# Output scaling on one engine and its sums on another, in a sketched attention and expert attention kernel

## The chip, the cores and the metric

The kernel runs on one core of a Trainium2 chip. The metric is the time on the device in microseconds (us). Before the change it was 341.58 us, the median of three runs (339.06 to 341.63).

The engines are named as the profile names them: PE is TensorE (matmuls; PEld its weight loads), DVE is VectorE, ACT is ScalarE, POOL is GpSimd, and SP is SyncE, which here only issues transfers. They run side by side, each through its own instructions in order, and wait for one another by semaphores. SBUF is the working memory, of 128 partitions. PSUM holds the results of the matmuls[...].

## The reference

Two blocks follow one another. The first is an attention whose queries and keys are sketched to 64 features; its output is the input `x` of the second, a causal attention with four experts, of which each token uses the best two.

```python
# 4 batches, 4 heads, 1088 tokens, head size 32, sketch size r = 8
def phi(x):
    a = np.einsum('rd,bhsd->bhsr', S1, x)
    b = np.einsum('rd,bhsd->bhsr', S2, x)
    return np.einsum('bhsi,bhsj->bhsij', a, b).reshape(*x.shape[:-1], r * r)
q_p, k_p = phi(q), phi(k)
kv = np.einsum('bhsf,bhsd->bhfd', k_p, v)
z = np.sum(k_p, axis=2)
num = np.einsum('bhsf,bhfd->bhsd', q_p, kv)
den = np.einsum('bhsf,bhf->bhs', q_p, z)[..., None] + 1e-06
attn_out = num / den                     # then (B, S, 128) as x

# 4 experts, expert size 64; w: shares of the best two experts of each token
...
for e in range(4):
    q = x @ wq[e]; k = x @ wk[e]; v = x @ wv[e]
    scores = scale * (q @ k.transpose(0, 2, 1))
    scores = np.where(causal, -1e9, scores)
    scores = scores - scores.max(-1, keepdims=True)
    a = np.exp(scores)
    a /= a.sum(-1, keepdims=True) + 1e-09
    ye = a @ v @ wo[e]
    for kk in range(2):
        out += (topk[:, :, kk] == e)[..., None] * w[:, :, kk:kk + 1] * ye
```

## The kernel before

All is float32. The four batches are pipelined: while a batch goes through the expert attention, the first block of the next batch is put between. The expert attention of a batch is a list of units. A unit holds the scores of up to two blocks of 128 queries and one pair of experts (index `g`, two pairs); two units with the same 256 queries (index `p`) make one output. A last unit has the 64 remaining queries.

Per unit, TensorE makes scores (`sc`), VectorE adds the mask and takes the maximum (`take`, L460), ScalarE makes exponentials and their sums `z` (`soften`, L466), TensorE turns the exponentials in blocks (`tp`, L86), these are copied out of PSUM (`aT`), TensorE multiplies them with the values (`av`, L590), the result is copied out (`yT`) and multiplied with the output weights (`po`, L662). A copy out of PSUM goes to VectorE or ScalarE by an account of the work booked on each:

```python
given = {"v": 0, "a": 0}
def evacuate(out_, in_, lean=-0):
    n = math.prod(in_.shape[1:])
    if given["v"] + lean + 70 < given["a"]:
        give("v", n + 100)
        nc.vector.tensor_copy(out_, in_)          # L74
    else:
        give("a", n + 30)
        nc.scalar.copy(out_, in_)                 # L77
```

The products of the sketch. In the first batch VectorE makes them, in the others GpSimd, in two pieces (`j0` to `j1` is 0 to 4 and 4 to 9), that is 1024 and 1280 columns:

```python
def sketch(nm, xT_, j0, j1):
    ...                                           # two sketches per token into abS (kab, qab)
    ab = abS[nm][:, :, j0:j1].rearrange("p x j h r -> p x (j h) r")
    n = H * (j1 - j0)
    with tc.issue_after(fps["turned"].ins) if first else nullcontext():
        ins = (nc.vector if first else nc.gpsimd).tensor_tensor(          # L293: kp, qp
            out=fps[nm][:, j0:j1].rearrange("p j h (x y) -> p (j h) x y", y=R),
            in0=ab[:, 1, :, None, :].to_broadcast([128, n, R, R]),
            in1=ab[:, 0, :, :, None].to_broadcast([128, n, R, R]),
            op=ALU.mult)
```

The share of an expert, divided by its sum of exponentials, is one number per token and expert:

```python
def shares(name, z, gws):
    r = p4.tile([128, 2, E], F32, tag="r", ...)
    nc.vector.tensor_scalar_add(r, z, 1e-9)                               # L556
    nc.vector.reciprocal(r, r)                                            # L557
    nc.vector.tensor_tensor(out=r, in0=r, in1=gws, op=ALU.mult)           # L558
    return r
```

It is made where the second unit of an output makes its values, just ahead of the `av` matmuls, and used when the output is made:

```python
def values():
    share = None if g < NG - 1 else shares(f"{b}_{p}", z, gw[:, 2 * p : 2 * p + 2])
    av = bank(f"av{name}")
    ...                                                                   # matmuls, L590
    evacuate(yT[:, g], av[:, 0:256])
    return [] if g < NG - 1 else [lambda: output(b, p, yT, share)]

def output(b, p, yT, share):
    nq, n = (128, 2) if p < NJ // 2 else (64, 1)
    final = b == B - 1 and p == 0
    pos = [bank(...) ... for e in range(2)]       # a bank for each expert of a pair
    acc = p2.tile([128, 2, NG, DM], F32, tag="acc", ...)[0:nq, 0:n]       # two buffers
    ...                                           # matmuls po, L662
    for g, x in [(g, x) for g in range(NG) for x in range(n)]:
        s0, s1 = (share[:, x, 2 * g + e : 2 * g + e + 1] for e in range(2))
        give("a", 260)
        give("v", 260)
        nc.scalar.activation(out=acc[:, x, g], in_=pos[0][:, x, g], func=ACTF.Copy, scale=s0)    # L668
        nc.vector.scalar_tensor_tensor(out=acc[:, x, g], in0=pos[1][:, x, g], scalar=s1,         # L669
                                       in1=acc[:, x, g], op0=ALU.mult, op1=ALU.add)
    ...
    for x in range(n) if final else [slice(0, n)]:
        eng = nc.vector if final else nc.gpsimd
        eng.tensor_tensor(out=ob[:, x], in0=..., in1=..., op=ALU.add)     # L675: sum over the pairs
        nc.sync.dma_start(out=tokens[:, x], in_=ob[:, x])
```

The order of VectorE's and ScalarE's instructions is that of the text, and comes from this loop over units (`done` are outputs, `tiled` and `cols` are parts of the next batch, such as sketches):

```python
made[0], exps = make(0)                           # scores, first block
emit(turns + rows); emit(exps)
made[1], exps = make(1)                           # scores, second block
emit(done)                                        # the output that came due
emit(tiled)
emit(exps[0:1]); emit(cols[0:2]); emit(exps[1:]); emit(cols[2:])
done = [f for values in group for f in values()]  # shares and values of the unit before
group = values
...
```

Of the kernel before, what the change touches and what calls it, by code (L numbers as in the profile page):

```python
# [10 lines left out]
F32 = mybir.dt.float32  # L11
# [8 lines left out]
def kernel(  # L20
# [201 lines left out]
    def prepare(b):  # L222
# [40 lines left out]
        def sketch(nm, xT_, j0, j1):  # L263


            if nm not in abS:
                abS[nm] = p2.tile([128, 2, NJ, H, R], F32, tag="ab", name=f"{nm}ab{b}")
                fps[nm] = p2.tile([128, NJ, H, R * R], F32, tag="fp", name=f"{nm}p{b}")

            w, parts = (32, NS) if first else (32 * NS, 1)  # L270
            ts = [bank(f"{nm}ps{b}_{j0}_{m}") for m in range(2)]
            for j in range(j0, j1):
                for m in range(2):
                    for half in (0, 64):
                        rows, x = slice(64 * m, 64 * m + 64), 128 * j + half
                        for s in range(parts):
                            nc.tensor.matmul(ts[m][half : half + 64, w * (j - j0) : w * (j - j0) + w],
                                             xT_[rows, x : x + 64],
                                             SKW[rows].rearrange("p s x h r -> p (s x h r)")[:, w * s : w * s + w],
                                             start=(s == 0), stop=(s == parts - 1))  # L280
            for m in range(2):
                t = ts[m][:, 0 : w * (j1 - j0)].rearrange("p (j s x d) -> p s x j d", j=j1 - j0, x=2, d=2 * R)
                part = abS[nm][:, :, j0:j1, 2 * m : 2 * m + 2].rearrange("p x j h r -> p x j (h r)")
                give("a", 16 * (j1 - j0) + 60)
                nc.scalar.copy(part, t[:, 0])
                if w > 32:
                    give("v", 16 * (j1 - j0) + 100)
                    nc.vector.tensor_tensor(out=part, in0=part, in1=t[:, 1], op=ALU.add)

            ab = abS[nm][:, :, j0:j1].rearrange("p x j h r -> p x (j h) r")  # L290
            n = H * (j1 - j0)
            with tc.issue_after(fps["turned"].ins) if first else nullcontext():
                ins = (nc.vector if first else nc.gpsimd).tensor_tensor(  # L293
                    out=fps[nm][:, j0:j1].rearrange("p j h (x y) -> p (j h) x y", y=R),
                    in0=ab[:, 1, :, None, :].to_broadcast([128, n, R, R]),
                    in1=ab[:, 0, :, :, None].to_broadcast([128, n, R, R]),
                    op=ALU.mult)
            if first:
                mark[0] = ins.ins

# [261 lines left out]
    def units(b, qk, vt, gw):  # L562

        of_tiles = {}

        def tiles(p):
            if p not in of_tiles:
                of_tiles[p] = (p2.tile([128, NG, 256], F32, tag="yT", name=f"yT{b}_{p}"),  # L570
                               p4.tile([128, 2, E], F32, tag="z", name=f"z{b}_{p}"))
            return of_tiles[p]

        def weights(p, g):
            return p2.tile([128, 16 * 256], F32, tag="aT", name=f"aT{b}_{p}_{g}")

        def group(p, g, aT):
            yT, z = tiles(p)
            nk = 2 * (2 * p + 2)
            aT = aT[:, 0 : nk * 256].rearrange("p (e j s) -> p e j s", e=2, s=256)  # L580
            name = f"{b}_{p}_{g}"

            def values():
                share = None if g < NG - 1 else shares(f"{b}_{p}", z, gw[:, 2 * p : 2 * p + 2])
                av = bank(f"av{name}")
                for j in range(2 * p + 2):
                    lo = 128 * max(0, j - 2 * p)
                    for e in range(2):
                        c = HD * (2 * g + e)
                        nc.tensor.matmul(av[HD * e : HD * e + HD, lo:256], vt[:, j, c : c + HD],  # L590
                                         aT[:, e, j, lo:256], start=(j == 0), stop=(j == 2 * p + 1))

                evacuate(yT[:, g], av[:, 0:256])
                if g < NG - 1:
                    return []
                return [lambda: output(b, p, yT, share)]

            def make(x):
                return scores(b, 2 * p + x, g, qk, z[:, x, 2 * g : 2 * g + 2])

            def turns(made, x):
                return turns_of(f"{name}_{x}", 2 * p + x, made[x], aT, 128 * x)

            return "P" if p == 1 else "G", make, turns, [values]

        def first_group():
            yT, z = tiles(0)
            aT = weights(0, 0)
            four = [group(0, g, aT[:, 4 * 256 * g :]) for g in range(NG)]
            return ("Q", lambda x: scores_first(b, qk, [z[:, :, 2 * g : 2 * g + 2] for g in range(NG)]),  # L610
                    lambda made, x: [f for g in range(NG) for i in range(2) for f in turns_of(
                        f"{b}_0_{g}_{i}", i, made[0][g][i], aT[:, 4 * 256 * g :][:, 0 : 4 * 256].rearrange(
                            "p (e j s) -> p e j s", e=2, s=256), 128 * i)],
                    [four[g][3][0] for g in range(NG)])

        large = [(p, g) for p in ((1, 2, 3) if b < B - 1 else (1, 3, 2)) for g in range(NG)]
        last_at = large.index((3, 1))
        if b < B - 1:
            yield first_group()
        last_at = large.index((3, 1))  # L620
        for n, (p, g) in enumerate(large):
            yield group(p, g, weights(p, g))
            if n == last_at:
                yield last_unit(b, qk, vt, gw)
        if b == B - 1:
            yield first_group()

    def last_unit(b, qk, vt, gw):
# [3 lines left out]
        z_all = p4.tile([64, 1, E], F32, tag="z8a", name=f"za{b}_8", bufs=2)  # L632
        yT = p2.tile([128, NG, 256], F32, tag="yT", name=f"yT{b}_8")

        def values():
            av = bank(f"av{b}_8")
            for g in range(NG):
                for j in range(NJ):
# [4 lines left out]
                                         aT[0:m, e, j, 64 * g : 64 * g + 64], start=(j == 0), stop=(j == NJ - 1))  # L643

            evacuate(yT[:, :, 0:64], av[:, 0:128].rearrange("p (g s) -> p g s", g=NG))
            for g in range(NG):
                nc.vector.tensor_copy(z_all[:, 0, 2 * g : 2 * g + 2], z[64 * g : 64 * g + 64])
            share = shares(f"{b}_8", z_all, gw[0:64, NJ - 1 : NJ])
            return [lambda: output(b, NJ // 2, yT, share)]

        return ("L", lambda x: scores_last(b, qk, z), lambda made, x: turns_of(f"{b}_8", NJ - 1, made[0], aT, 0), [values])

    def output(b, p, yT, share):

        nq, n = (128, 2) if p < NJ // 2 else (64, 1)
        final = b == B - 1 and p == 0
        pos = [bank(f"po{b}_{p}_{e}").rearrange("p (x g d) -> p x g d", x=2, g=NG)[0:nq] for e in range(2)]
        acc = p2.tile([128, 2, NG, DM], F32, tag="acc", name=f"acc{b}_{p}")[0:nq, 0:n]
        for g, x in [(g, x) for g in range(NG) for x in range(n)]:
            for e in range(2):  # L660
                rows = slice(64 * e, 64 * e + 64)
                nc.tensor.matmul(pos[e][:, x, g], yT[rows, g, 128 * x : 128 * x + nq], wo_sb[rows, g],  # L662
                                 start=True, stop=True)
        for g, x in [(g, x) for g in range(NG) for x in range(n)]:
            s0, s1 = (share[:, x, 2 * g + e : 2 * g + e + 1] for e in range(2))
            give("a", 260)
            give("v", 260)
            nc.scalar.activation(out=acc[:, x, g], in_=pos[0][:, x, g], func=ACTF.Copy, scale=s0)  # L668
            nc.vector.scalar_tensor_tensor(out=acc[:, x, g], in0=pos[1][:, x, g], scalar=s1, in1=acc[:, x, g],  # L669
                                           op0=ALU.mult, op1=ALU.add)  # L670
        ob = p2.tile([128, 2, DM], F32, tag="ob", name=f"ob{b}_{p}")[0:nq, 0:n]
        tokens = out[b, 256 * p : 256 * p + nq * n, :].rearrange("(x p) d -> p x d", p=nq)
        for x in range(n) if final else [slice(0, n)]:
            eng = nc.vector if final else nc.gpsimd
            eng.tensor_tensor(out=ob[:, x], in0=acc[:, x, 0] if final else acc[:, :, 0],  # L675
                              in1=acc[:, x, 1] if final else acc[:, :, 1], op=ALU.add)
            nc.sync.dma_start(out=tokens[:, x], in_=ob[:, x])

    with tc.manual_schedule(engines={mybir.EngineType.PE}):

# [16 lines left out]
        for b in range(B):  # L697
            coming, ahead, later = prepare(b + 1) if b + 1 < B else (None, {}, {})
            for n, (kind, make, turned, values) in enumerate(units(b, *now)):
# [6 lines left out]
                exps = []  # L706
                if kind in "PG":
                    made[1], exps = make(1)
                emit(done)
                emit(tiled)  # L710

# [1 line left out]
                emit(cols[0:2])  # L713
                emit(exps[1:])
                emit(cols[2:])
                done = [f for values in group for f in values()]
                group = values
                turns = [f for x in made for f in turned(made, x)]
                n = (len(turns) + 1) // 2
# [1 line left out]
                turns = turns[n:]  # L721
            now, own = coming, later
        emit(turns + done)
        emit([f for values in group for f in values()])
        order.close()


# [28 lines left out]
```

## Time and profile before

| | before |
|---|---|
| time, median of three runs | 341.58 us |
| span of the profiled run | 335.9 us |
| PE busy | 320.7 us |
| DVE busy | 267.9 us |
| ACT busy | 225.8 us |
| POOL busy | 45.9 us |
| TensorE clock granted | 0.999 |

The profile is one execution on the chip. A group of instructions is given by line, engine, operation, output and inputs by their names in the program, shape and count; then its busy time, the mean of one in ns, and the idle time of the engine just before it with what ended that idle time. In the timeline each line is start and length in us, engine, line, operation, tiles and count, with the idle time before it in brackets where there was any; consecutive instructions of one kind are merged. The chain is followed back from the last instruction, at each step to what released it or to the instruction before it on its engine. Matmuls are pipelined and their ends are modelled, so a busy PE need not be at its peak.

### The profile page before, as it was taken

Reading aid. Unit: us, or ns where it says so; the run is one execution under the profiler, and the core shown is the slowest. Engines: PE = TensorE matmul, PEld = TensorE weight load, DVE = VectorE, ACT = ScalarE, POOL = GpSimd, SP = SyncE. Lnnn points to the kernel's source line nnn. Section 1 sums busy time; section 2 is a strip of 40 time slices with the busy share of each in tenths; the row PEclk is TensorE's granted clock in tenths of the full one; section 3 lists DMA queues with packets and bytes.
Section 4 is the critical chain, followed back from the end, with each engine's and each line's share of the span. In section 5 each row is a group of like instructions: output and inputs, shape, how many; then the busy total and the mean of one; then the engine's idle time right before and its main releaser. Section 6 shows DMA issues by size and latency. Waiting matters only on the chain.

```text
span 335.9 us, 12306 instructions
## 1 busy us (share of the span) xinstructions
PE 320.7 (95%) x5130; PEld 223.0 (66%) x5130; DVE 267.9 (80%) x886; ACT 225.8 (67%) x607; POOL 45.9 (14%) x60
## 2 busy tenths in 40 slices
PE   8989999999999989999999989999999999989993
PEld 3846658777657658767666656887766665757672
DVE  6758899897684999987866699989768668768774
ACT  1448676877576767665855866697757768855863
POOL 4000156000000243300000050500000000000000
PEclk9999999999999999999999999999999999999999
DMA  7352221300000202000000000000000000000001
GB/s 203 63 165 46 74 99 43 85 4 2 19 0 3 86 4 86 4 19 2 18 2 2 19 6 17 4 18 3 4 17 2 2 23 0 16 4 2 19 6 32
DMA packets 11384, 10.23 MB, mean 30 GB/s; under 512 B 3648, under 2 KB 10304, under 8 KB 11328
## 3 DMA queue, kind: packets, MB, share of 16 engines
q1 hardware_dynamic: 11312, 9.45, 10.3%
q8 instruction: 40, 0.66, 0.8%
q14 instruction: 16, 0.13, 0.1%
q10 hardware_dynamic: 16, 0.00, 0.0%
HBM read 7.22 MB, written 2.23 MB: 28 GB/s over the span
## 4 chain that ended last, share of the span: by engine, by line
PE 78%; DVE 13%; ACT 6%; issue 2%; DVEq 0%
PE av L590 18%; PE sc L480 15%; PE tp L86 10%; PE qk L369 7%; PE po L662 5%; PE vg L385 4%; ACT a L466 3%; PE kv L311 3%; PE num L337 2%; ACT aT L77 2%; PE sc L522 2%; DVE a L460 2%; PE warm L683 2%; DVE acc L669 2%; PE av L642 2%
## 5 line engine op out<-in xcount | busy, mean ns | idle before, releaser
L466 ACT ACTIVATE a<-a,mx 128x128 f32<-128x128 f32 (+8 forms) x136 | 108.3, 809 | 10.2 <-DVE mx L460 10.1
L77 ACT COPY aT<-tp 128x512 f32<-128x512 f32 (+6 forms) x162 | 68.5, 493 | 50.1 <-PE tp L86 49.2
L460 DVE CUSTOM_DVE_ANT_0 a<-sc,mask 128x512 f32<-128x512 f32 (+3 forms) x136 | 74.1, 591 | 8.6 <-PE sc L480 4.3
L480 PE MATMUL sc<-qkT 64*128 64x512 f32 (+3 forms) x320 | 78.2, 540 | 0.6 <-DVE yT L74 0.6
L590 PE MATMUL av<-aT,vt 128*64 128x256 f32 (+1 forms) x640 | 70.5, 360 | 1.6 <-ACT aT L77 1.4
L590 PEld LDWEIGHTS av<-aT,vt 128*64 128x64 f32 x640 | 46.8, 137 | 26.8 <-issue 3.8
L86 PEld LDWEIGHTS tp<-ident,a 64*128 64x128 f32 x1296 | 49.3, 138 | 11.0 <-issue 5.4
L86 PE MATMUL tp<-ident,a 64*128 64x64 f32 x1296 | 55.5, 226 | 0.2 <-ACT vt L77 0.2
L480 PEld LDWEIGHTS sc<-qkT 64*128 64x128 f32 x320 | 35.7, 188 | 17.5 <-DVE mx L460 6.1
L675 POOL TENSOR_TENSOR ob<-acc 128x256 f32<-128x256 f32 (+1 forms) x19 | 12.8, 671 | 239.3 <-DVE acc L669 208.2
L74 DVE COPY aT<-tp 128x320 f32<-128x320 f32 (+5 forms) x54 | 26.4, 530 | 21.1 <-PE tp L86 20.9
L460 DVE CUSTOM_DVE_ANT_0 a<-sc,mask,mx 128x512 f32<-128x512 f32 (+3 forms) x72 | 38.3, 568 | 0.0
L369 PE MATMUL qk<-xT,wqk 128*64 128x512 f32 x128 | 32.3, 602 | 0.7 <-ACT xT L77 0.7
L662 PEld LDWEIGHTS po<-wo,yT 64*128 64x128 f32 (+1 forms) x288 | 21.1, 181 | 10.8 <-DVE yT L74 5.6
L466 ACT ACTIVATION_READ_ACCUMULATOR a<-a,mx 128x1 f32 x136 | 27.9, 205 | 0.0
L662 PE MATMUL po<-wo,yT 64*128 64x128 f32 (+1 forms) x288 | 23.5, 279 | 3.7 <-DVE yT L74 3.7
L669 DVE SCALAR_TENSOR_TENSOR acc<-po,r,acc 128x128 f32<-128x128 f32 (+1 forms) x72 | 20.4, 343 | 7.1 <-ACT acc L668 7.0
L668 ACT ACTIVATE acc<-po,r 128x128 f32<-128x128 f32 (+1 forms) x72 | 20.6, 366 | 2.3 <-PE po L662 2.0
L74 DVE COPY yT<-av 128x256 f32<-128x256 f32 (+1 forms) x23 | 9.0, 391 | 15.1 <-PE av L590 12.7
L77 ACT COPY yT<-av 128x256 f32<-128x256 f32 x13 | 4.8, 374 | 22.4 <-PE av L590 22.4
L385 PE MATMUL vg<-wvg,xT 128*64 128x260 f32 x136 | 18.2, 391 | 0.0
L460 DVE DVE_READ_ACCUMULATOR2_ANT mx<- 128x1 f32 x216 | 17.8, 82 | 0.0
(118 smaller groups left out, 337.2 us busy)
## 6 DMA issues: line engine op xcount, KB each, us to landing
kin<-in_k_dram SPq DMA_DIRECT2D x4, 544.0 KB, 3.7
qin<-in_q_dram SPq DMA_DIRECT2D x4, 544.0 KB, 4.0
vin<-in_v_dram SPq DMA_DIRECT2D x16, 128.0 KB, 5.5
out_dram<-ob SPq DMA_DIRECT2D x15, 128.0 KB, 1.8
vtl<-in_v_dram SPq DMA_DIRECT2D x8, 16.0 KB, 2.7
wqk<-in_moe_wq_dram SPq DMA_DIRECT2D x1, 128.0 KB, 5.2
wqk<-in_moe_wk_dram SPq DMA_DIRECT2D x1, 128.0 KB, 3.2
wvg<-in_moe_wv_dram SPq DMA_DIRECT2D x1, 128.0 KB, 3.3
```

Of the source, the lines that this page charges most:

```text
L74: nc.vector.tensor_copy(out_, in_)
L77: nc.scalar.copy(out_, in_)
L86: nc.tensor.transpose(ts[half][0 : in_.shape[1], 64 * x : 64 * x + 64], in_[rows], ident[rows, rows])
L369: nc.tensor.matmul(t[64 * e : 64 * e + 64], wqk[:, a // NG, 2 * (a % NG) + e], xT[:, 512 * c : 512 * c + 512], start=True, stop=True)
L385: nc.tensor.matmul(t[x : x + 64, 0 : E * HD + E], xT[:, 128 * j + x : 128 * j + x + 64], wvg, start=True, stop=True)
L460: nc.vector.tensor_tensor_reduce(out=dst, in0=src, in1=msk, scale=-1.0, scalar=most, op0=ALU.add, op1=ALU.min, accum_out=mx)
L466: nc.scalar.activation(out=a, in_=a, func=ACTF.Exp, bias=mx, scale=-1.0, accum_out=z)
L480: nc.tensor.matmul(sc[e], qk[rows, g, 128 * i : 128 * i + 128], qk[rows, NG + g, keys], start=True, stop=True)
L590: nc.tensor.matmul(av[HD * e : HD * e + HD, lo:256], vt[:, j, c : c + HD], aT[:, e, j, lo:256], start=(j == 0), stop=(j == 2 * p + 1))
L662: nc.tensor.matmul(pos[e][:, x, g], yT[rows, g, 128 * x : 128 * x + nq], wo_sb[rows, g], start=True, stop=True)
L668: nc.scalar.activation(out=acc[:, x, g], in_=pos[0][:, x, g], func=ACTF.Copy, scale=s0)
L669: nc.vector.scalar_tensor_tensor(out=acc[:, x, g], in0=pos[1][:, x, g], scalar=s1, in1=acc[:, x, g], op0=ALU.mult, op1=ALU.add)
```

## The change

There are three parts. The first takes the scaling of an output from ScalarE and VectorE together to VectorE alone: for each expert of a pair, one product of a whole PSUM bank with the shares, broadcast along the columns. GpSimd then adds the two experts, and after that the two pairs. The account books this on VectorE alone. The last output of the kernel keeps the old form. The second cuts GpSimd's sketch products into pieces of 256 columns, so that no single instruction of it is long. The third makes the shares ahead of the output that came due, instead of behind the sketches, except in the first two units of the first batch, where the gate is not ready by then. `acc` is twice as large and has one buffer instead of two.

```diff
@@ sketch
-            ab = abS[nm][:, :, j0:j1].rearrange("p x j h r -> p x (j h) r")
-            n = H * (j1 - j0)
...
+            for x0 in range(j0, j1, j1 if first else 1):
+                x1 = j1 if first else x0 + 1
+                ab = abS[nm][:, :, x0:x1].rearrange("p x j h r -> p x (j h) r")
+                n = H * (x1 - x0)
...
+                    ins = (nc.vector if first else nc.gpsimd).tensor_tensor(
+                        out=fps[nm][:, x0:x1].rearrange("p j h (x y) -> p (j h) x y", y=R),
...
@@ units
-            def values():
-                share = None if g < NG - 1 else shares(f"{b}_{p}", z, gw[:, 2 * p : 2 * p + 2])
+            def share():
+                return shares(f"{b}_{p}", z, gw[:, 2 * p : 2 * p + 2]) if g == NG - 1 else None
+
+            def values(share):
...
@@ output
-        acc = p2.tile([128, 2, NG, DM], F32, tag="acc", name=f"acc{b}_{p}")[0:nq, 0:n]
+        acc = p2.tile([128, 2, 2, NG, DM], F32, tag="acc", name=f"acc{b}_{p}", bufs=1)[0:nq, :, 0:n]
...
-            give("a", 260)
-            give("v", 260)
-            nc.scalar.activation(out=acc[:, x, g], in_=pos[0][:, x, g], func=ACTF.Copy, scale=s0)
-            nc.vector.scalar_tensor_tensor(out=acc[:, x, g], in0=pos[1][:, x, g], scalar=s1, in1=acc[:, x, g],
-                                           op0=ALU.mult, op1=ALU.add)
...
+        if final:
...                                               (as before, on ScalarE and VectorE)
+            return
+        for e in range(2):
+            give("v", 612)
+            nc.vector.tensor_tensor(
+                out=acc[:, e], in0=pos[e][:, 0:n], op=ALU.mult,
+                in1=share.rearrange("p x (g e) -> p x g e", g=NG)[:, :, :, e, None].to_broadcast([nq, n, NG, DM]))
+        nc.gpsimd.tensor_tensor(out=acc[:, 0], in0=acc[:, 0], in1=acc[:, 1], op=ALU.add)
+        nc.gpsimd.tensor_tensor(out=ob, in0=acc[:, 0, :, 0], in1=acc[:, 0, :, 1], op=ALU.add)
+        nc.sync.dma_start(out=tokens, in_=ob)
@@ loop over units
+                late = b == 0 and n < 2
+                if not late:
+                    group = [(share(), f) for share, f in group]
                 emit(done)
                 emit(tiled)
...
                 emit(cols[2:])
-                done = [f for values in group for f in values()]
+                if late:
+                    group = [(share(), f) for share, f in group]
+                done = [f for share, value in group for f in value(share)]
```

## The prediction

> **What bounds the kernel now.** I read the busy shares, then the chain that ended last, then the busy time in stretches of 20 us, then the timeline where TensorE is idle.
>
> ```profile
> PE 320.7 (95%) x5130; PEld 223.0 (66%) x5130; DVE 267.9 (80%) x886; ACT 225.8 (67%) x607; POOL 45.9 (14%) x60
> ...
> PE 78%; DVE 13%; ACT 6%; issue 2%; DVEq 0%
> ...
> L669 DVE SCALAR_TENSOR_TENSOR acc<-po,r,acc 128x128 f32<-128x128 f32 (+1 forms) x72 | 20.4, 343 | 7.1 <-ACT acc L668 7.0
> L668 ACT ACTIVATE acc<-po,r 128x128 f32<-128x128 f32 (+1 forms) x72 | 20.6, 366 | 2.3 <-PE po L662 2.0
> ```
>
> TensorE (PE) carries the span: 335.9 - 320.7 leaves 15.2 us of open idle time. Yet 21% of the chain (VectorE, ScalarE, issue; 70 us) is not matmul, so some matmuls are held while they count as busy. The gain can come only from places where VectorE or ScalarE makes TensorE late. The stretches name one (stretch, length, busy us of PE, weight loads, DVE, ACT, POOL, then clock and DMA):
>
> ```profile
> 100.00:120.00 20.00, 19.41 (x339) 13.76 (x335) 14.67 (x54) 13.93 (x51) 4.32 (x4) 1.00 0.13 39
> 120.00:140.00 20.00, 18.28 (x322) 14.07 (x321) 19.69 (x58) 13.42 (x39) 7.38 (x6) 1.00 0.12 36
> 140.00:160.00 20.00, 19.81 (x381) 14.51 (x379) 16.49 (x54) 13.92 (x34) 0.73 (x1) 1.00 0.04 10
> ```
>
> From 120 to 140 VectorE is busy 19.69 of 20 us, GpSimd has its products, and TensorE loses 1.72 us. The stretch 200 to 220 looks alike (19.69 and 18.48). Part of "busy" is waiting, as the timeline shows:
>
> ```profile
> 116.83 4.29 POOL L293 TENSOR_TENSOR kp<-kab 128x1024 f32<-128x1024 f32 x2
> ...
> 119.04 2.12 DVE L556 TENSOR_SCALAR r<-z 128x8 f32<-128x8 f32 x1
> ...
> 121.19 0.20 DVE L557 RECIPROCAL r<-r 128x8 f32<-128x8 f32 x1
> 121.43 0.17 DVE L558 TENSOR_TENSOR r<-r,gw 128x8 f32<-128x8 f32 x1
> 121.51 0.42 DVE L74 COPY yT<-av 128x256 f32<-128x256 f32 x1
> ...
> 121.98 1.16 PE L662 MATMUL po<-wo,yT 64*128 64x128 f32 x16 [1.67 <-DVE yT L74]
> ```
>
> An addition on 8 columns takes 2.12 us, where its median is 0.166 us, and ends when the second GpSimd product ends (116.83 + 4.29 = 121.12). The copy of yT behind it is late, and TensorE stands 1.67 us. The same happens 80 us later (199.08, 2.12 us; TensorE idle 1.50 us). In the first batch it looks worse on VectorE:
>
> ```profile
> 53.70 1.35 DVE L556 TENSOR_SCALAR r<-z 128x8 f32<-128x8 f32 x1
> 55.08 0.20 DVE L557 RECIPROCAL r<-r 128x8 f32<-128x8 f32 x1
> 55.31 2.08 DVE L558 TENSOR_TENSOR r<-r,gw 128x8 f32<-128x8 f32 x1
> ```
>
> but the chain there is TensorE's without a break (kv, av, tp, sc from 52.59 to 60.42), so these 3.1 us are hidden.
>
> [...] the addition on SBUF (L556) and the product of two SBUF tiles (L558) stretch to the end of a GpSimd instruction, and the reciprocal between them, with GpSimd still busy, took its normal 0.20 us. [...] L346, PSUM times a broadcast, took 419 ns for 256 columns and 485 ns for 320, 1.03 ns a column. [...] Here it is 1.59 times: 1950 ns against 1227 ns for the 1024-column sketch product. [...]
>
> **The outputs.** There are 19 outputs besides the last (15 of 128 rows and two column blocks, 4 of 64 rows and one), and only these change.
> Removed on ScalarE: 15 x 4 + 4 x 2 = 68 activations at 366 ns = 24.9 us busy. Removed on VectorE: 68 scalar_tensor_tensors at 343 ns = 23.3 us.
> Added on VectorE: 30 products of 128x512. From L346: 419 + 256 x 1.03 = 683 ns each; with 8 of 64x256 at 419 ns, 20.5 + 3.4 = 23.9 us. So VectorE's own work is even (+0.6 us). What changes is that the product does not wait for ScalarE: L669 waited 7.0 us in all.
> Added on GpSimd: the existing additions took 730 ns for 256 columns and 450 ns for 128 (64 rows), 2.2 ns a column; 512 columns are then 1.29 us. 15 x 1.29 + 4 x 0.73 = 22.3 us, off the path except at the end.
> Moved: the kernel books 612 twice on VectorE's account and nothing on ScalarE's for an output, in place of 260 four times on both, so its balancing of PSUM copies tips. By the order of instructions of the changed kernel, 24 copies (154 to 130 on VectorE, 9,944 columns) go to ScalarE. At about 0.49 us (530 ns mean for aT there) that is 12 us off VectorE and about as much onto ScalarE: ScalarE falls by some 13 us, VectorE by 11 us.
> Where it counts is the boundary of a batch. The chain there (start, length in us, what):
>
> ```profile
> 107.00 1.95 ACT a L466 x9
> 108.95 0.26 ACT acc L668
> 109.21 0.03 issue
> 109.24 1.13 DVE acc L669 x4
> 110.36 0.59 DVE qkT L74
> 110.96 1.15 DVE kT L244
> ```
>
> VectorE had ended its score reductions at 106.57 and sat 2.66 us behind eight exponentials for the activations at 108.85. The output matmuls had ended by 106. In the new form the products start at once, and a qkT copy of 0.6 us goes to ScalarE.
>
> **The sketch products in pieces.** Per sketch on GpSimd two instructions (1.95 + 2.39 us, 4.31 us in sequence) become nine of 256 columns. The slope is (2.39 - 1.95) / 256 = 1.72 ns a column, so a piece is 1950 - 768 x 1.72 = 0.63 us, nine are 5.7 us, and over six sketches GpSimd gets 8 us more. With the additions, GpSimd comes to 45.9 + 22.3 + 8 = 76 us, 23%. A blocked VectorE instruction then waits 0.6 us at most, not 2.1.
>
> **The shares ahead of the outputs.** Nothing is added. The addition, reciprocal and product move ahead of the previous output and of the sketch's additions, so before GpSimd gets its next sketch. The stretched L556 and L558 add up to 10.5 + 8.4 us for 16 each against 0.166 and 0.167 us normal; the excess is 13.5 us, of which 13 us should go.
>
> **The sum.** VectorE falls from 268 by 13 + 11 - 0.6 to about 244 us, ScalarE from 226 to 213. TensorE does the same work in the same order, so little of that shows in the time. On the path:
> - Two boundaries with sketches behind them (105 to 122, 185 to 202): VectorE's string of kT, yT, score reductions, output, kab, qT, yT starts about 2 us sooner, bounded by the scores on TensorE, and at its end the 2.1 us wait goes. TensorE can use only what it lacks: 0.55 us at 112.47, and then the scores at 119.24, which hold it for 0.85 us (eight of these matmuls took 1.77 us at 81.14, four took half), so that with the 0.55 us the output matmuls could start at 119.5 in place of 121.98. I take 2.4 us each, 4.8 us together.
> - The stretch after the third output of a batch, where VectorE's aT copies stand on the chain at 64.86 (1.67 us) and 224.61 (1.27 us); near 144 the chain stays on TensorE. A lighter ScalarE takes some of these copies; a guess of 0.5 us in each batch, 1.5 us.
> - Diffuse holds elsewhere: 0.8 us, a guess.
> - The end: acc has one buffer now, so the last output's activation must wait for GpSimd to finish the output before it: products done near 329.2, plus 1.29 and 0.73 is 331.2 us, where the activation started at 331.02. The last shares, 0.64 us at 329.64 already, meet the same additions. Loss 0.5 us.
>
> Sum: 4.8 + 1.5 + 0.8 - 0.5 = 6.6 us, and 341.6 - 6.6 = 335.0 us.
>
> **Rivals.** (a) TensorE is the bound and absorbs it: the idle gaps of 1.67 and 1.50 us are all that counts, and the rest of the chain is only one of several equal ones. 95% busy and the hidden stall at 53.7 us speak for it; then 338 us. (b) The bound was VectorE in more places than the chain shows: with 24 us off it, holds inside the score bursts shrink throughout, and the time is 330 us. The saturated stretches speak for it; the others, at 13 to 17 of 20 us, against. (c) GpSimd becomes a new wait: in the first batch kp would follow output additions of 2.0 us and then take 5.7 us, from 44.2 to about 52, and its matmuls start at 52.59; 0.6 us off and TensorE waits, at the tail likewise. [...] Then 341 to 343 us. The spare time in later batches (sketch done near 122, used from 131) speaks against more than a microsecond.
>
> **Range and chances.** The predicted time is 335.0 us, between (a) and (b). The three runs of before spread by 2.6 us, so I take 330.5 to 339.5. Two per cent is 6.8 us, just above my sum: faster by more 0.43, within 0.53, slower 0.04.
>
> **What would show it.** Right: no L556-type instruction above 0.8 us except at the end, VectorE near 244 us, the 1.67 and 1.50 us gaps gone, products of 512 columns near 0.68 us, GpSimd near 76 us. Wrong: products well above 0.7 us, TensorE waiting for kp, or a boundary-to-boundary time (119.04 to 199.08 before, 80.0 us) that has not shrunk by 2 us or more.

## The result and the profile after

The changed kernel took 328.69 us (median of four runs, 328.34 to 328.94); the kernel before, beside it, 340.32 us. The ratio is 0.9666, with a 95% interval of 0.9599 to 0.9733: 3.3% faster, and 1.8 us below the range that was predicted.

Busy time, the chain's shares, and the two groups that are new, from the page of the kernel after:

```profile
PE 314.5 (96%) x5130; PEld 219.5 (67%) x5130; DVE 248.2 (76%) x832; ACT 218.6 (67%) x563; POOL 73.8 (23%) x121
...
PE 88%; DVE 4%; ACT 4%; issue 2%; POOL 0%; POOLq 0%; DVEq 0%
...
L689 POOL TENSOR_TENSOR acc<-acc 128x512 f32<-128x512 f32 (+1 forms) x19 | 22.0, 1159 | 205.2 <-DVE acc L686 194.7
...
L686 DVE TENSOR_TENSOR acc<-po,r 128x512 f32<-128x512 f32 (+1 forms) x38 | 22.3, 627 | 0.3 <-issue 0.3
```

In the first of these lines each engine has its busy time in us, its share of the span and its number of instructions; PEq, DVEq and POOLq are an engine's own sequencer. VectorE's share of the chain is down from 13% to 4%. The products (L686) wait for nobody, where the old form waited 7 us. The stretches, in the columns of the prediction:

```profile
100.00:120.00 20.00, 20.00 (x354) 14.63 (x351) 16.02 (x58) 14.33 (x49) 6.84 (x11) 1.00 0.14 39
120.00:140.00 20.00, 20.00 (x360) 15.07 (x358) 15.69 (x53) 14.38 (x39) 11.48 (x18) 1.00 0.13 37
140.00:160.00 20.00, 19.26 (x372) 14.01 (x370) 16.85 (x54) 15.07 (x32) 0.64 (x1) 1.00 0.03 10
```

From 120 to 140 us VectorE has gone from full to 15.69 of 20 us, and TensorE is busy without a gap, although GpSimd now works 11.5 us there. The timeline around the place where TensorE had stood:

```profile
113.68 0.17 DVE L558 TENSOR_SCALAR r<-z 128x8 f32<-128x8 f32 x1
113.88 0.20 DVE L559 RECIPROCAL r<-r 128x8 f32<-128x8 f32 x1
...
114.12 0.17 DVE L560 TENSOR_TENSOR r<-r,gw 128x8 f32<-128x8 f32 x1
...
116.31 5.29 POOL L295 TENSOR_TENSOR kp<-kab 128x256 f32<-128x256 f32 x9
...
118.81 1.05 PE L669 MATMUL po<-wo,yT 64*128 64x128 f32 x16
```

The shares are done 2 us before GpSimd begins its products, and the output matmuls have no idle time in brackets. Ahead of them the chain is TensorE's alone:

```profile
104.57 0.95 PE po L669 x16
105.51 1.87 PE qk L371 x8
107.38 2.54 PE av L651 x72
109.92 0.52 PE tp L86 x10
```

But for the order of the matmuls inside an output, TensorE's instructions follow one another as before, so the starts of the same matmuls show where the 8.7 us between the two profiled spans (335.9 and 327.2) came from:

| start of (us) | before | after | difference |
|---|---|---|---|
| po of the fourth output, first batch | 104.81 | 104.40 | -0.41 |
| po behind the first boundary | 121.98 | 118.81 | -3.17 |
| po at the end of its sketches | 139.45 | 135.24 | -4.21 |
| po of the fourth output, second batch | 184.59 | 180.02 | -4.57 |
| po behind the second boundary | 202.02 | 194.44 | -7.58 |
| po at the end of its sketches | 219.95 | 210.87 | -9.08 |
| the last po but one | 326.67 | 317.58 | -9.09 |
| the last po | 329.77 | 320.07 | -9.70 |
| end of the span | 335.9 | 327.2 | -8.7 |

The first boundary (104.81 to 139.45) gave 3.8 us, the second (184.59 to 219.95) 4.5 us, the 107 us from there to the last output nothing, and the end took 1 us back:

```profile
320.21 1.27 POOL L689 TENSOR_TENSOR acc<-acc 128x512 f32<-128x512 f32 x1 [10.34 <-DVE r L558]
320.42 1.08 DVE L560 TENSOR_TENSOR r<-r,gw 128x8 f32<-128x8 f32 x1
321.56 0.72 POOL L690 TENSOR_TENSOR ob<-acc 128x256 f32<-128x256 f32 x1
322.31 1.14 ACT L677 ACTIVATE acc<-po,r 128x128 f32<-128x128 f32 x4 [1.75 <-POOL ob L690]
```

In brackets is the idle time before an instruction and what ended it. The last share product is held by GpSimd's sum (1.08 us), and the last activations wait 1.75 us for the one buffer of `acc`.

### The profile page after: what moved, and what is told of

It reads as the page before. It is cut to its first block, busy times and chain, and to the rows that moved or that the text cites. A ratio compares the mean times of both kernels' runs of the same rounds, so it can differ in the third digit from the quotient of the medians.

```text
span 327.2 us, 12289 instructions
## 1 busy us (share of the span) xinstructions
PE 314.5 (96%) x5130; PEld 219.5 (67%) x5130; DVE 248.2 (76%) x832; ACT 218.6 (67%) x563; POOL 73.8 (23%) x121
## 4 chain that ended last, share of the span: by engine, by line
PE 88%; DVE 4%; ACT 4%; issue 2%; POOL 0%; POOLq 0%; DVEq 0%
PE av L594 19%; PE sc L482 18%; PE tp L86 12%; PE qk L371 9%; PE po L669 5%; PE vg L387 5%; PE av L651 3%; PE kv L313 3%; PE num L339 3%; PE sc L524 2%; ACT aT L77 2%; PE warm L697 2%; PE kps L277 2%; PE sc L500 2%; PE qps L277 1%
## 5 line engine op out<-in xcount | busy, mean ns | idle before, releaser
L77 ACT COPY aT<-tp 128x512 f32<-128x512 f32 (+6 forms) x171 | 71.9, 492 | 63.5 <-PE tp L86 63.3
L482 PE MATMUL sc<-qkT 64*128 64x512 f32 (+3 forms) x320 | 73.7, 537 | 0.0
L689 POOL TENSOR_TENSOR acc<-acc 128x512 f32<-128x512 f32 (+1 forms) x19 | 22.0, 1159 | 205.2 <-DVE acc L686 194.7
L86 PEld LDWEIGHTS tp<-ident,a 64*128 64x128 f32 x1296 | 48.0, 138 | 11.4 <-issue 6.1
L86 PE MATMUL tp<-ident,a 64*128 64x64 f32 x1296 | 53.7, 226 | 0.2 <-ACT vt L77 0.2
L482 PEld LDWEIGHTS sc<-qkT 64*128 64x128 f32 x320 | 33.0, 188 | 14.9 <-issue 5.9
L74 DVE COPY aT<-tp 128x320 f32<-128x320 f32 (+5 forms) x45 | 22.6, 536 | 14.8 <-PE tp L86 14.4
L686 DVE TENSOR_TENSOR acc<-po,r 128x512 f32<-128x512 f32 (+1 forms) x38 | 22.3, 627 | 0.3 <-issue 0.3
L295 POOL TENSOR_TENSOR qp<-qab 128x256 f32<-128x256 f32 x27 | 15.9, 627 | 11.8 <-DVE qab L288 11.8
L371 PEld LDWEIGHTS qk<-xT,wqk 128*64 128x64 f32 x128 | 9.7, 136 | 11.3 <-issue 6.7
```

Of the source, the lines that this page charges most:

```text
L86: nc.tensor.transpose(ts[half][0 : in_.shape[1], 64 * x : 64 * x + 64], in_[rows], ident[rows, rows])
L371: nc.tensor.matmul(t[64 * e : 64 * e + 64], wqk[:, a // NG, 2 * (a % NG) + e], xT[:, 512 * c : 512 * c + 512], start=True, stop=True)
L482: nc.tensor.matmul(sc[e], qk[rows, g, 128 * i : 128 * i + 128], qk[rows, NG + g, keys], start=True, stop=True)
L686: nc.vector.tensor_tensor(out=acc[:, e], in0=pos[e][:, 0:n], op=ALU.mult, in1=share.rearrange("p x (g e) -> p x g e", g=NG)[:, :, :, e, No ...
L689: nc.gpsimd.tensor_tensor(out=acc[:, 0], in0=acc[:, 0], in1=acc[:, 1], op=ALU.add)
```

## The experiments

Two theories stood against each other. The hold theory: the loss was VectorE held by GpSimd at the two boundaries, and what piled up behind it. The load theory: the gain is ScalarE's and VectorE's lighter work. In the expectations of e1 to e7, a figure without a theory's name is the hold theory's. The kernel before had medians of 338.31, 338.75, 337.98 and 338.54 us beside the four groups of runs (e1 to e4, e5 to e8, e9 to e11, e12 to e14). Ratios are to it. They leave out executions more than 1.5% above the fastest of their kernel; the medians do not.

### One part alone

**e1: the shares ahead, nothing else.**

```diff
+                late = b == 0 and n < 2
+                if not late:
+                    group = [(share(), f) for share, f in group]
                 emit(done)
                 emit(tiled)
...
```

> Only the shares are moved ahead; outputs and sketch products as before. [...] (the loss was VectorE held by GpSimd's sketch products at the two batch boundaries with sketches, and the backlog behind it): most of the gain is here, the time falls by 5 to 7 us of the full change's 11.6, no share instruction is above 0.7 us, and the stretch 119 to 141 us gets some 3 us shorter. Load theory (ScalarE's 68 activations and the copies that move off VectorE made the gain): at most 2 us.

Measured: 331.95 us, ratio 0.983 (0.978 to 0.988). The held shares at the boundaries are gone. From the matmuls' starts, the first boundary became 2.1 us shorter and the second 2.9 us. The hold theory stands: this part alone gives some 6 us of the medians.

**e3: pieces of 256, nothing else.**

```diff
-            ab = abS[nm][:, :, j0:j1] ...
+            for x0 in range(j0, j1, j1 if first else 1):
+                x1 = j1 if first else x0 + 1
...
```

> Only the sketch products in pieces of 256; shares and outputs as before. [...] a held share instruction waits for one piece, 0.6 us, instead of 2.1, so about 1.4 us come back at each of the two boundaries, 2 to 4 us together. Load theory: nothing, within 1 us. A third possibility: VectorE is held once by each of several pieces and the 2 us stay.

Measured: 333.26 us, ratio 0.986 (0.982 to 0.990). The share instructions of this kernel (count, then shortest, median and longest in ns):

```profile
L560 DVE TENSOR_TENSOR r<-r,gw x20: 153/166/308, 40.4 to 326.3; 128x8 f32<-128x8 f32 x16, 64x4 f32<-64x4 f32 x4
```

The products that were held for 2.08 us now take 0.31 us, and the addition at the boundary 0.19 us. This is more than the 2 to 4 us expected: one piece costs so little that nearly the whole wait goes.

**e2: the outputs in the new form, nothing else.**

```diff
-            nc.scalar.activation(out=acc[:, x, g], ...); nc.vector.scalar_tensor_tensor(...)
+            nc.vector.tensor_tensor(out=acc[:, e], in0=pos[e][:, 0:n], in1=(share, broadcast), op=ALU.mult)
+        nc.gpsimd.tensor_tensor(out=acc[:, 0], in0=acc[:, 0], in1=acc[:, 1], op=ALU.add)
```

> Only the outputs in the new form (products on VectorE, sums on GpSimd, account of 612 twice); shares and sketch products where they were. Load theory: 6 us or more of the 11.6. [...] 2 to 3 us, because the share instructions still stretch to 2 us behind the sketch products at 119 and 199 us, and GpSimd's longer queue can make them stretch more.

Measured: 337.94 us, ratio 0.997 (0.994 to 1.000), so next to nothing. The timeline of an execution of 342.19 us at the first boundary:

```profile
115.76 4.29 POOL L295 TENSOR_TENSOR kp<-kab 128x1024 f32<-128x1024 f32 x2
...
116.56 3.53 DVE L558 TENSOR_SCALAR r<-z 128x8 f32<-128x8 f32 x1
...
120.91 0.91 PE L482 MATMUL sc<-qkT 64*128 64x512 f32 x1 [1.96 <-DVE yT L74]
```

VectorE came to the share at 116.56, 2.5 us sooner than in the kernel before, and then lay 3.53 us instead of 2.12, to the end of the second product, although it began in the first. Of what it had won it waited 1.4 us away; the other 1.1 us reached the output matmuls (120.92 for 121.98). The rest of the loss lies behind the hold, where TensorE was granted less of its clock than in the kernel before (1.00 in both stretches; the clock is third from the right):

```profile
120.00:130.00 10.00, 9.09 (x54) 5.34 (x56) 6.81 (x18) 3.79 (x10) 2.05 (x3) 0.66 0.21 63
200.00:210.00 10.00, 8.04 (x42) 4.62 (x40) 8.18 (x16) 4.18 (x10) 4.17 (x3) 0.66 0.00 0
```

That is up to (0.34 + 0.34) x 10 = 6.8 us of TensorE's time, an estimate. Of the 22 executions the two with a mean clock of 0.997 took 335.50 and 335.99 us, where the kernel before took 337.40 to 338.53 us at 0.997 to 0.999. At equal clock the new outputs alone are therefore worth some 2 us, as the hold theory had it; the median hides it.

**e4: the kernel before again.** No edit.

> The kernel before, unchanged, to see where its executions differ (337.8 to 341.6 us, while the changed kernel's lie within 0.6 us). [...] the longer executions have longer or more held share instructions, or a held one where the shorter have none. Otherwise the difference lies somewhere else, for example in the loads of the first batch, and the share instructions look the same in both.

Measured: 338.06 us, ratio 1.000 (0.998 to 1.001). The held shares are the same to within 0.03 us. The profiled execution is 1.2 us longer than the first one, and the whole of it arose between the matmuls that started at 202 and 210 us, where the granted clock (0.83) is lower; in the first it was 1.00:

```profile
202.00:212.00 10.00, 10.00 (x128) 6.29 (x132) 9.08 (x28) 6.22 (x18) 0.73 (x1) 0.83 0.05 14
```

So the spread of the kernel before does not lie in the length of the holds, but at least here in the granted clock. The 341.58 us from which the prediction started was about 3 us above what the same kernel took later.

### One part left out

**e5: without the pieces.**

```diff
-            for x0 in range(j0, j1, j1 if first else 1):
-                x1 = j1 if first else x0 + 1
+            for x0 in (j0,):
+                x1 = j1
```

> The changed kernel with the sketch products again in two long pieces: outputs new, shares ahead. Shares alone gave 6.4 us and pieces alone 5.1 us, which are not additive if both remove the same wait. [...] with the shares ahead nothing is left for the pieces to shorten; the time is that of the full change within 0.7 us (328.5 to 329.5). If the pieces also help elsewhere (other instructions held, kv earlier), it is 1 us or more slower.

Measured: 328.55 us, ratio 0.971 (0.967 to 0.975), the time of the full change. Once the shares are ahead, the pieces do nothing.

**e7: with the old outputs.** The block of `output` is that of the kernel before.

> The changed kernel with the outputs in the old form on ScalarE and VectorE: shares ahead, pieces of 256. [...] as with shares alone, 331.5 to 332.3 us, so the new outputs are worth some 3 us once the waits are gone, though they were worth 0.4 us alone. Load theory gives the same sum but not the small value alone.

Measured: 332.17 us, ratio 0.980 (0.977 to 0.984), as with the shares alone. The new outputs are worth 332.17 - 328.55 = 3.6 us here, and were worth 0.4 us by themselves (some 2 us at equal clock, see e2).

**e6: without the shares ahead.** `share` is made at the head of `values`, as before.

> The changed kernel with the shares back behind the sketches: outputs new, pieces of 256. [...] each share instruction is held by one piece at most, so the 3.5 us waits of the outputs-only kernel become below 0.9 us and the time is 330 to 331.5 us, 1 to 2.5 us above the full change. If the place of the shares matters beyond the hold, it stays above 332 us.

Measured: 342.59 us, ratio 1.008 (1.005 to 1.011), some 2.7 us slower. This went against both theories: two parts that are harmless or good alone lose time together.

```profile
115.14 0.46 POOL L692 TENSOR_TENSOR ob<-acc 64x128 f32<-64x128 f32 x1
115.56 5.30 POOL L295 TENSOR_TENSOR kp<-kab 128x256 f32<-128x256 f32 x9
116.01 0.41 DVE L74 COPY yT<-av 128x256 f32<-128x256 f32 x1
116.35 4.54 DVE L558 TENSOR_SCALAR r<-z 128x8 f32<-128x8 f32 x1
```

One addition on 8 columns was passed over by eight pieces in a row and ended 0.03 us after the last. The pieces bound a hold in e3 but not here; they made it longer than in e2, because nine of them take 5.30 us and two long products 4.29 us. Still the output matmuls behind this boundary start at 121.73, no later than in the kernel before (121.98). What is lost is lost behind the holds, again at a lower clock:

```profile
120.00:130.00 10.00, 8.28 (x76) 5.35 (x78) 8.19 (x21) 3.79 (x10) 2.87 (x4) 0.83 0.20 63
200.00:210.00 10.00, 7.25 (x44) 4.63 (x46) 7.83 (x17) 3.31 (x9) 3.90 (x6) 0.66 0.00 0
```

That is up to (0.17 + 0.34) x 10 = 5.1 us of TensorE's time, an estimate, where the span (339.2) is 3.3 us above that of the kernel before. All 14 executions had a mean clock of 0.989 or less; the kernel before beside them had up to 0.999. So the holds alone do not make this loss; the lower clock behind them does, as far as the estimate goes. Where in e2, e4 and e6 the clock fell at a boundary, TensorE had stood 1.5 to 3.0 us there; in the profiled executions of the changed kernel and of e1, e3, e5, e7 and e8 it stood at most 0.6 us on end there and lost no clock. That the one brings the other is not shown: the profiled execution of the kernel before also stood 1.67 and 1.50 us, and its clock stayed at 1.00.

**e8: with the old account.** The products stay; the copies stay where they were.

```diff
-            give("v", 612)
+            give("v", 260 * len(parts) // 2)
+            give("a", 260 * len(parts) // 2)
```

> The changed kernel whose account books 1040 on both engines for an output, as before, so that all 154 copies on VectorE stay there (154 and 218, none of 24 moved). It splits the outputs' 3 us: if the gain comes from VectorE not waiting for ScalarE behind its exponentials, the time stays within 0.7 us of the full change; if it comes from the 24 moved copies, it is 1.5 to 3 us slower, near 331 us.

Measured: 331.37 us, ratio 0.980 (0.975 to 0.984): 2.8 us above e5. So most of the outputs' 3.6 us comes from the 24 copies that move to ScalarE, into the room that the activations left; what is left for VectorE no longer waiting is 0.8 us by these medians, 1.3 us by the spans (330.3 for e7, 329.0 for e8). The end hides part of the second: the last output's matmuls start at 324.23 (e7), 322.18 (e8) and 319.47 us (e5), so up to there no longer waiting gave 2.1 us and the copies 2.7 us, and behind it the new form loses 0.7 us from e7 to e8.

### What makes a hold long

**e10 and e11: probes.** Additions of 128x8 in SBUF on a scratch tile, 48 in all, behind the sketches. They add work, and held probes delay what is behind them; the times of these kernels (345.85 and 343.80 us) tell nothing else.

```diff
+    def probe():
+        if probes[0] > 0:
+            probes[0] -= 1
+            nc.vector.tensor_scalar_add(pout, pin, 1e-9)
...
```

> The changed kernel with eight extra additions of 128x8 in SBUF on VectorE (a scratch tile, nothing reads it) behind each pair of sketch parts on GpSimd, each after a copy or a score reduction: 48 probes at many moments of the nine pieces. If a hold ends with the GpSimd instruction that runs, no probe takes over 0.65 us. If a probe can be passed over, as the share addition was in the kernel without the shares ahead (4.5 us, eight pieces), some take several pieces; then the moment within a piece, or the instruction before the probe, should tell which.

> The same 48 probes with the sketch products in two long pieces. If a hold ends with the running instruction: probes of up to 2.4 us, and none beyond the end of the first piece when it began in the first. If it can be passed over: some that began in the first piece end with the second, up to 4.3 us, as the share addition of 3.5 us with the outputs alone did.

The probes of e10 (pieces) and then of e11 (long products), again shortest, median and longest in ns:

```profile
L87 DVE TENSOR_SCALAR pout<-pin x48: 153/161/4526, 46.2 to 228.2; 128x8 f32<-128x8 f32 x48
```

```profile
L87 DVE TENSOR_SCALAR pout<-pin x48: 135/160/3526, 45.9 to 226.2; 128x8 f32<-128x8 f32 x48
```

In e10 two probes were passed over by eight pieces (4.53 and 4.52 us), in e11 two by both products (3.53 and 3.52 us), each time one at the kp made during the second batch and one during the third. No other probe took over 0.65 us at a piece, or outlasted the long product in which it began. The two long ones of e10 began 0.21 us into a piece; a probe at the kp made during the first batch, 0.19 us into a piece, took 0.47 us, so the moment within a piece hardly decides. What the long ones share is the GpSimd instruction ahead of kp: the sum of a 64-row output, on half of the partitions, as in the fence of e6.

**e12 and e13: the half instruction taken away, and put elsewhere.**

```diff
 e12
-        nc.gpsimd.tensor_tensor(...)                     # both sums
+        eng = nc.gpsimd if nq == 128 else nc.vector
+        eng.tensor_tensor(...)
 e13
+            if not first and nm == "q" and j1 == NJ:
...
+                nc.gpsimd.tensor_tensor(out=hbuf[0:64], in0=part, in1=part, op=ALU.add)   # 64x160, not used
```

> The kernel with pieces and 48 probes, but the two sums of the 64-row outputs on VectorE, so that GpSimd runs nothing on only half of the partitions ahead of kp in the second and third batch, where one probe each was held through eight pieces (4.5 us). [...] no probe is now held above 0.7 us but behind the long vp copy. If the long hold comes from the moment within a piece or from the copy before the probe, one of 4 us or more stays at kp of these batches.

> The kernel with pieces and 48 probes, and a further GpSimd sum on 64 rows (160 columns, into a scratch tile nobody reads) put between the fourth and fifth piece of each qp. At qp no probe was held above 0.65 us by pieces so far. If a half instruction makes the long holds, probes that begin in the fifth to ninth piece of qp are now held to the end of the last piece (and into the vp copy behind it), 1 to 3 us; if not, they stay at 0.65 us. The two long ones at kp stay in either case.

Without the half instruction (e12, one execution, 335.25 us) the probes are:

```profile
L87 DVE TENSOR_SCALAR pout<-pin x48: 133/194/1019, 46.2 to 217.7; 128x8 f32<-128x8 f32 x48
```

The longest, 1.02 us, is behind one vp copy of 1.05 us; none at a piece takes over 0.65 us. (The edit also moved the probes: at kp of the later batches the first now began 1.69 us into the string, not 0.80 us.) With a half instruction in the middle of qp (e13, 355.43 us), where no hold had passed one piece:

```profile
57.40 0.44 POOL L303 TENSOR_TENSOR hbuf<-qab 64x160 f32<-64x160 f32 x1
57.75 4.04 DVE L88 TENSOR_SCALAR pout<-pin 128x8 f32<-128x8 f32 x1
57.81 2.95 POOL L309 TENSOR_TENSOR qp<-qab 128x256 f32<-128x256 f32 x5
60.71 1.04 POOL L251 COPY vp<-vin 128x1024 f32<-128x1024 f32 x1
```

The probe outlasted the five pieces and the vp copy, 4.04 us; in the two later batches one took 3.72 and one 2.72 us. So the half instruction makes the long hold here, and every hold of these runs that lasted through several pieces, or ran on from the first long product through the second, had one directly ahead of the string of full ones. It is not the whole condition. In e3 a half instruction is there too, and the share addition was let in at the end of the fourth piece:

```profile
115.99 0.45 POOL L683 TENSOR_TENSOR ob<-acc 64x128 f32<-64x128 f32 x1 [5.20 <-issue]
116.40 5.28 POOL L295 TENSOR_TENSOR kp<-kab 128x256 f32<-128x256 f32 x9
118.61 0.19 DVE L558 TENSOR_SCALAR r<-z 128x8 f32<-128x8 f32 x1
```

It began 2.21 us into the string; the long holds all began within 0.81 us of the start of theirs. Whether that is what is missing no run tests, and how the half instruction acts no run shows.

### The end

**e9 and e14: nothing for GpSimd at the end.** The output before the last keeps the old form, with its sums on VectorE; e14 also books it.

```diff
-        if final:
+        if final or (b == B - 1 and p == 2):
             for g, x in parts:
                 ...
+                if p:                       # e14 alone
+                    give("v", 306)
```

> The changed kernel, but the output just before the last keeps the old form too, with its sums on VectorE, so that GpSimd has nothing to do at the end. In the changed kernel the last share product is held 1.08 us by GpSimd's sum and the last activation waits 1.75 us for acc. If these two waits set the end, the time falls by 0.7 to 1.3 us, to 327.4 to 328.0; if the matmuls or the transfer set it, it stays within 0.3 us of 328.7.

Measured: 329.49 us, ratio 0.974 (0.972 to 0.976), no gain. Both waits are gone, but unbooked work tipped the account, and the last two yT copies came to VectorE, behind the sums:

```profile
321.09 0.49 PE L669 MATMUL po<-wo,yT 64*128 64x128 f32 x4 [1.21 <-DVE yT L74]
```

> As the kernel with the old form for the output just before the last, but with 1224 booked on VectorE for it, so that the last yT copies stay on ScalarE: there they had moved to VectorE behind the sums, and TensorE stood 1.57 us. If the hold and the wait for acc are then gone without a new wait, 327.5 to 328.2 us, 0.5 to 1 us below the changed kernel; if ScalarE's four activations delay the copies as much, 328.5 to 329.

Measured: 327.84 us (327.40 to 328.23), ratio 0.967 (0.963 to 0.971), the lowest median of all, though the ratio is that of the full change. The span is 325.7 us, and the last chain holds no GpSimd:

```profile
318.13 1.14 ACT acc L677 x4
319.28 0.27 ACT yT L77
319.55 0.04 issue
319.59 1.37 PE po L669 x16
320.96 0.36 ACT acc L677
```

The last activations start 1.37 us behind their matmuls, 2.24 us in the changed kernel (320.07 to 322.31): 0.87 us, which is the 0.85 us between the medians. The medians stem from different groups of runs and the ratios are the same, so the gain rests on the trace.

## Why the prediction was wrong, point by point

**The start.** The gain was predicted as 6.6 us and taken off 341.58 us. But the execution whose profile was read took 337.67 us, and the same kernel took 338.0 to 338.8 us later. Some 3 to 4 us of the 6.3 us between 335.0 and 328.69 are this; the profiled spans differ by 8.7 us, 2.1 us more than predicted. Beside the later medians the changed kernel is about 2.9% faster. The signs named for being right came (VectorE's 248.2 us least closely); from one boundary's output matmuls to the next (118.81 to 194.44 in place of 121.98 to 202.02) it is 4.4 us less.

**Costs of single instructions: right.** Products 683 ns, measured 685; 409 ns on 64 rows for 419. That no hold would lengthen them was assumed, and none of the 38 took over 693 ns. Sums on GpSimd 1.29 us, measured 1.275. A piece 0.63 us, measured 0.625, though nine followed each other in 5.3 us, not 5.7. GpSimd 73.8 us for 76.

**Busy totals: VectorE 248.2 for 244, ScalarE 218.6 for 213.** The sum took durations off a busy time in which they overlap. Four activations had 366 ns each but took 1.12 us together, 0.28 us apiece: 68 x 0.28 = 19 us, not 24.9. With the 12 us of copies that is 225.8 - 19 + 12 = 218.8 us.

**The boundaries, 2.4 us each: the term that failed.** They gave 3.8 and 4.5 us. The mechanism was the one named: the share addition held by the sketch products (2.12 us at each boundary), VectorE waiting for ScalarE, then TensorE for yT. Its size was not. The time between the starts of the same matmuls, in us at the first and the second boundary, shows where:

| from, to | before | e1 (shares alone) | e8 (old account) | after |
|---|---|---|---|---|
| fourth output, output of 64 rows | 8.82, 9.30 | 9.03, 9.30 | 7.94, 7.95 | 7.95, 7.94 |
| output of 64 rows, output behind kp | 8.35, 8.13 | 6.47, 6.47 | 6.48, 6.47 | 6.46, 6.48 |
| output behind kp, end of the sketches | 17.47, 17.93 | 17.01, 16.70 | 16.72, 16.95 | 16.43, 16.43 |

The hold at kp (second row) gave 1.9 and 1.7 us, as large as was thought (2.4 less the 0.55 us ahead of it). Two things were too small. Ahead of it only the open gap of 0.55 us was counted, and 0.9 and 1.4 us came back: matmuls held while they count as busy gave the rest, and it was the new outputs that freed them (e8 has this gain, e1 and e7 have not). Behind it the prediction set nothing, and 1.0 and 1.5 us came, of them 0.5 and 1.2 us by the shares alone. There VectorE had been held 3.4 us by the products of qp (132.56 to 136.24, and again from 213.04), a hold that e1 takes away too. The prediction names such a hold for the first batch alone, as hidden, and hidden it was: e1 changed that stretch by 0.2 us.

**"A lighter ScalarE takes some of these copies", 1.5 us: right in place, too small in the whole.** The stretch after the third output gave 0.64, 0.46 and 0.19 us, 1.3 us. But e8 shows the moved copies worth 2.8 us of the medians; they also work at the boundaries, where the prediction spoke of one qkT copy. The 0.8 us of diffuse holds did not come: from 220 to 326 us the difference stayed at 9.1 us.

**The end, 0.5 us lost: right.** From 9.09 us to 8.7 us is 0.4 us lost, by the two waits named; e14 takes them away and gets 0.9 us.

**"A blocked VectorE instruction then waits 0.6 us at most": wrong in general.** It was an estimate from the length of a piece, 0.63 us. It held in e3 (0.64 us at most), and in e6 the wait was 4.54 us. In the full change it doesn't matter, because the shares are ahead. It does decide what the parts are worth: shares alone 6.4, pieces alone 5.1, outputs alone 0.4 us (some 2 at equal clock), and outputs with pieces lose 2.7 us, at a lower clock.

**The rivals.** (a) is out: more than the two open gaps came back. (b), VectorE the bound in more places than the chain shows, has its number nearest (330 us), but not its reason: the places are the boundaries it shared with the prediction, and elsewhere only the stretches after the third outputs shrank, by 1.3 us in all. (c), GpSimd as a new wait, is out for kp and right for the end.

## What to carry to other kernels

When a tiny VectorE instruction on SBUF ends each time with a GpSimd instruction beside it, move it ahead of that work in VectorE's order before anything else: here this alone gave 6 us, and shortening GpSimd's instructions on top of it nothing. A wait that ends at an event elsewhere swallows part of what is won ahead of it (1.4 of 2.5 us in e2), so remove the last wait of a string first. Before calling a part useless or harmful, compare executions of equal granted clock (e2, e6). Move a cost from one engine to another together with the account that balances them: the moved copies were worth at least as much as the waits that went (e8), and one unbooked output lost its gain (e9).

## What the runs showed of the hardware

A VectorE addition of 128x8 in SBUF took 0.17 us in the median, and in places much longer beside GpSimd's sketch products. Beside the pieces of 0.62 us in e10 the probes took 0.65 us at most, but for two. Where a 64-partition GpSimd instruction ran directly ahead of the string and the addition began within 0.81 us of the string's start, it was passed over to the end: 4.5 us over eight pieces (e6, e10), 3.5 us over two long products (e2, e11), up to 4.04 us over five pieces and a copy (e13). Where it began 2.21 us into such a string, it ended with the instruction that ran: 2.12 us in the kernel before, 0.19 us in e3. A reciprocal of the same size on the same tile took 0.20 us beside a running product (at 55.08, 133.92 and 214.43 us of the kernel before). Behind the boundaries of e2 and e6 the granted clock of TensorE was 0.66 to 0.83 over 10 us, and 1.00 in the same stretches of the changed kernel.
